# Second layer of all batches but the first with seven quarter products instead of eight, in a fused top-k attention and mixer kernel

## The chip, the cores and the metric

The kernel runs on one core of a Trainium2 chip. The metric is the device time of one execution in microseconds; lower is better. The core's engines work side by side, each through its own list of instructions in order: PE (TensorE) multiplies matrices and writes to PSUM, DVE (VectorE), ACT (ScalarE) and POOL (GpSimd) work on rows of 128 partitions, and SP issues nearly all DMAs of this kernel. [...]

## The reference

Eight batches, eight heads, 576 rows, 64 columns a head. Per head the scores are cut to the 32 largest of each row, then softmax and the product with the values follow; the heads side by side are x, 576 x 512 a batch. Then x is mixed along the rows with a matrix of rank 32, and a two-layer network with ReLU (512 to 2048 to 512) follows, with a residual:

```python
scores = scale * np.matmul(q, k.transpose(0, 1, 3, 2))
kth = np.partition(scores, -top_k, axis=-1)[..., -top_k:-top_k + 1]
scores = np.where(scores >= kth, scores, -1000000000.0)
...
h = x.transpose(0, 2, 1) @ U @ V
u = x + h.transpose(0, 2, 1)
return u + np.maximum(u @ w_ch1, 0.0) @ w_ch2
```

Left out above are the softmax, the product with v and the bridge that puts the heads side by side as x. Everything is fp32.

## The kernel before, in words

**Attention.** It goes by pairs of heads: group g is pair g % 4 of batch g // 4, 32 groups in all. A group has five steps t: four of 128 rows and a last one of 64. The main loop at the end of the file runs over steps n = 5g + t and writes the order of all engines out by hand (a manual schedule: every engine runs its instructions in the order of the program; only the waits are put in automatically, from what reads and writes a tile). In one step stand, from several groups and steps at once: scores of the next step (PE, L323, evicted by ACT, L351), `fold` and `split`, which make a larger half and a smaller half of each row for the search (POOL L390, then DVE L392, then POOL L393), the search for the 32 largest (DVE, `front`: L432 to L463), the marking of what lies below the 32nd (ACT L488, POOL L491), the exponentials (ACT L397), the transposed blocks of the weights (DVE L518, then by SP to DRAM and back: four `away` writes L524 and one `PT` read L528), and the products with the values (PE, L571 to L585, evicted at L594). At t = 0 `load` issues the 21 loads of the next group on SP (L247 to L280). `mixed` (L597) makes the mixer's input u of a pair, transposed: `uT`, 512 x 576 a batch.

**The two layers.** When the last pair of a batch is mixed, `mlp(b)` goes to the list `fillers`. It is a generator that writes one matmul at a time and yields what it costs. `fill`, called eight times in a step, adds a share to `due` and takes matmuls until it is used up; so the layers of one batch are spread between the attention work of the next 20 steps. What is left after the last step runs alone: all of batch 7, and a rest of batch 6.

A batch's 576 columns of uT are cut into two spans of 320 and 256 (`SPAN`). For each span the first layer makes 16 blocks of 128 hidden rows: 4 matmuls (L656) into a PSUM tile `mm`, then ReLU by ACT into SBUF (`hT`, L668). The second layer makes 4 blocks `c` of 128 output rows: 16 matmuls (L675) into an `mm` tile. There are two `mm` tiles, each of 512 fp32 columns, one PSUM bank. The result is copied by ACT and the residual added by POOL (L690, L691); in batch 7 DVE adds from PSUM at once (L688). `turned_back` (L696) transposes a block and stores it: by PE and ACT (L723 to L734), or in batch 7, but for the last block, by DVE and eight or twelve small DMAs (L705 to L717). These jobs wait in the list `late` until the fifth ReLU of the next span or the thirteenth matmul of the next block.

Each fp32 matmul with its weights shows as two matmul records and two weight loads.

**Setting-up.** Weights come as pairs of 32-bit words (`f64_raw`) through three tiles `raw` of 512 KB and are joined on ACT, DVE and POOL in batch 0's attention (L174 to L189).

Of the kernel before, what the change touches and what calls it, by code (L numbers as in the profile page):

```python
# [8 lines left out]
F32 = mybir.dt.float32  # L9
U8 = mybir.dt.uint8  # L10
U32 = mybir.dt.uint32
AF = mybir.ActivationFunctionType
ALU = mybir.AluOpType
# [13 lines left out]
def kernel(  # L27
# [28 lines left out]
    nc = tc.nc  # L56
    B, H, S, D = q.shape
    P = 128
    C = H * D
    R = moe_U.shape[1] // 2  # L60
    F = moe_w_ch1.shape[1] // 2
    NF, NC = F // P, C // P
    NT, TAIL = 4, 64
    MAIN = NT * P
# [9 lines left out]
    NV = 3  # L74

    BLK = 32
    HT = 10
    PE, ACT = mybir.EngineType.PE, mybir.EngineType.Activation
    DVE, POOL, SP = mybir.EngineType.DVE, mybir.EngineType.Pool, mybir.EngineType.SP

# [480 lines left out]
    def values(g, t):  # L561

        PT = PTs.pop((g, t))
        va, vd, vt = (a[g % NV] for a in (vas, vds, vts))
        O = ps_t.tile([P, P], F32, tag="tp", name="O")
        if t == NT:
            den, x = dens[g], xs[g % 2]
            if g not in inverted:
                inverse(g, 2 * NT if g == NPAIR - 1 else 0, 2 * NT + 1)
            for j in range(NT + 1):  # L570
                nc.tensor.matmul(  # L571
                    O,
                    lhsT=PT[:, j],
                    rhs=va[:, :, j, :] if j < NT else vt,
                    start=(j == 0),
                    stop=(j == NT),
                )
            for h in range(2):
                nc.scalar.mul(x[half(h), NT, half(h)], O[half(h), half(h)], den[half(h), 2 * NT :])
            return  # L580
        nc.tensor.matmul(O, lhsT=vd, rhs=PT[:, 2 * NT], start=True, stop=False)  # L581
        PB = PT[:, 0 : 2 * NT].rearrange("p (a h) (c j) -> p h c a j", h=2, c=NT)
        for j in range(NT):
            for h in range(2):
                nc.tensor.matmul(  # L585
                    O[half(h)],
                    lhsT=va[:, h, j, :],
                    rhs=PB[:, h, j] if shared(g, t) else PT[:, NT * h + j],
                    start=False,
                    stop=(j == NT - 1),  # L590
                )
        if t == 0:
            XTs[g] = attn.tile([P, MAIN], F32, tag="XT", name="XT")
        nc.scalar.copy(XTs[g][:, cols(t)], O)  # L594


    def mixed(g, wait, lag=0):  # L597
# [45 lines left out]
        if gi == NPAIR - 1:  # L643
            fillers.append(mlp(b))

    def mlp(b):

        uT = uTs.pop(b)
        late = []
        for chunks, (lo, hi) in zip(PARTS, SPAN):  # L650
            w = hi - lo
            hTs = []
            for f in range(NF):
                ph = ps_m.tile([P, C], F32, tag="mm", name="mm")
                for cc in range(NC):
                    nc.tensor.matmul(  # L656
                        ph[:, 0:w],
                        lhsT=w1[:, cc, f * P : (f + 1) * P],
                        rhs=uT[:, cc, lo:hi],
                        start=(cc == 0),  # L660
                        stop=(cc == NC - 1),
                    )
                    if cc < NC - 1:
                        yield w / C
                if f % 2 == 0:
                    hT = mlpp.tile([P, 2, WIDE], F32, tag="hT", name="hT", bufs=HT)
                    hTs += [hT[:, 0], hT[:, 1]]
                nc.scalar.activation(hTs[f][:, 0:w], ph[:, 0:w], AF.Relu)  # L668
                if f == 4 and late:
                    late.pop()()  # L670
                yield w / C
            for c in range(NC):
                po = ps_m.tile([P, C], F32, tag="mm", name="mm")
                for f in range(NF):
                    nc.tensor.matmul(  # L675
                        po[:, 0:w],
                        lhsT=w2[:, f, c * P : (c + 1) * P],
                        rhs=hTs[f][:, 0:w],
                        start=(f == 0),
                        stop=(f == NF - 1),  # L680
                    )
                    if f == 12 and late:
                        late.pop()()
                    if f < NF - 1:
                        yield w / C
                oT = mlpp.tile([P, WIDE], F32, tag="oT", name="oT")
                if b == B - 1:
                    nc.vector.tensor_tensor(oT[:, 0:w], uT[:, c, lo:hi], po[:, 0:w], ALU.add)  # L688
                else:
                    nc.scalar.copy(oT[:, 0:w], po[:, 0:w])  # L690
                    nc.gpsimd.tensor_tensor(oT[:, 0:w], oT[:, 0:w], uT[:, c, lo:hi], ALU.add)  # L691
                late.append(turned_back(b, chunks, lo, c, oT))
                yield w / C
        late.pop()()

    def turned_back(b, chunks, lo, c, oT):  # L696

# [50 lines left out]
    def fill(k=1):  # L748
# [3 lines left out]
        for _ in range(k):  # L752
            if passes:
                passes.pop(0)()
            if mixing and next(mixing[0], True):
                mixing.pop(0)
            due += share * (SHORT if t == NT else 1) * (EARLY if n <= 2 * ALONE + 2 else 1)
            while due > 0:
                if not fillers:
                    due = 0.0  # L760
# [137 lines left out]
        fill(2)  # L898
    while mixing or fillers:
        fill()  # L900


# [29 lines left out]
```

## Time and profile before

| what | us |
|---|---|
| median of 3 runs (1717.31 to 1718.37) | 1718.03 |
| the profiled execution | 1716.65 |
| its span, first to last instruction | 1714.9 |
| PE busy | 1613.5 |
| DVE busy | 1484.2 |
| ACT busy | 1023.3 |
| POOL busy | 944.9 |
| L656, first layer, 2048 records, busy | 522.8 |
| L675, second layer, 2048 records, busy | 529.5 |
| q1, the queue of nearly all DMAs: share of 16 engines | 37.2% |

A group line in the profile reads: line, engine, operation, tiles written and read, shapes and count; then busy us and mean ns of one; then the idle time of the engine just before, and what ended it. The view of waits gives, for an engine and a line, whose end it waited for: us in total, times, longest. The timeline gives start, length, engine, line, operation and count, with the idle time before in brackets. The view by stretches gives the busy time of PE, PEld (weight loads), DVE, ACT and POOL, then PE's granted clock, the DMA engines' share and GB/s. [...]

### The profile page before, as it was taken

The page shows a single profiled execution, that of the slowest core. Times are in us where ns is not written, and L with a number is a line of the kernel's source. Part 1 is how long each engine was busy: PE and PEld are TensorE (multiplying, and loading weights), DVE is VectorE, ACT ScalarE, POOL GpSimd, SP SyncE. Part 2 cuts the span into 40 slices and gives each one's busy share as a digit, 9 for nine tenths or more (in the row PEclk, how much of TensorE's full clock was granted, in tenths as well). Part 3 has the DMA queues.
Part 4 walks back from the last instruction along what each step waited for, and adds up shares of the span by engine and source line. Part 5 has one row for each costly group of instructions (what it writes and reads, how often), then busy time and mean ns, then how long its engine had stood idle before and what let it go on. Part 6 is the DMA issues. An engine that isn't in the chain of part 4 may idle for free.

```text
span 1714.9 us, 29637 instructions
## 1 busy us (share of the span) xinstructions
PE 1613.5 (94%) x9489; PEld 1219.8 (71%) x9489; DVE 1484.2 (87%) x4317; ACT 1023.3 (60%) x2582; POOL 944.9 (55%) x749
## 2 busy tenths in 40 slices
PE   4666799998999999999999999999999999999999
PEld 2444566787777877788677877788677877788777
DVE  7999989999999999999999999999999999992000
ACT  4888797665656556565656566565655566563100
POOL 4778578666555555565555555565555555552000
PEclk7777899999999999999999999999999999999999
DMA  3322322344444444444444444444444444432010
GB/s 87 95 84 84 84 78 61 77 123 122 108 112 112 117 117 106 112 116 114 115 109 111 119 112 108 114 113 114 111 108 120 118 108 114 106 93 71 3 16 13
DMA packets 275837, 167.37 MB, mean 98 GB/s; under 512 B 173920, under 2 KB 260192, under 8 KB 275680
## 3 DMA queue, kind: packets, MB, share of 16 engines
q1 hardware_dynamic: 274624, 165.20, 37.2%
q8 instruction: 75, 1.23, 0.3%
q14 instruction: 82, 0.67, 0.1%
q10 hardware_dynamic: 1056, 0.26, 0.1%
HBM read 101.42 MB, written 63.96 MB: 96 GB/s over the span
## 4 chain that ended last, share of the span: by engine, by line
PE 71%; DVE 19%; SPq 3%; ACT 2%; issue 2%; DMA 2%; POOL 1%; POOLq 0%; DVEq 0%; ACTq 0%
PE mm L656 27%; PE mm L675 21%; PE sc L323 8%; DVE upper L458 6%; PE O L585 6%; DVE m L463 6%; DVE first L446 2%; SPq L252 2%; PE tp L551 1%; PE O L571 1%; SPq L247 1%; PE up L631 1%; PE O L581 1%; PE tp L546 1%; DVE y L518 1%
## 5 line engine op out<-in xcount | busy, mean ns | idle before, releaser
L675 PE MATMUL mm<-hT,w 128*128 128x256 f32 (+1 forms) x2048 | 529.5, 407 | 0.0
L656 PE MATMUL mm<-uT,w 128*128 128x256 f32 (+1 forms) x2048 | 522.8, 407 | 0.0
L491 POOL TENSOR_TENSOR Ssb<-Ssb,E 128x576 f32<-128x576 f32 x271 | 379.2, 1417 | 246.2 <-ACT E L488 245.8
L656 PEld LDWEIGHTS mm<-uT,w 128*128 128x128 f32 x2048 | 380.0, 191 | 97.6 <-issue 2.6
L675 PEld LDWEIGHTS mm<-hT,w 128*128 128x128 f32 x2048 | 377.9, 191 | 93.0 <-issue 2.9
L463 DVE MAX8 m<-upper 128x8 f32<-128x304 f32 (+1 forms) x864 | 407.7, 508 | 3.6
L458 DVE MATCH_REPLACE8 upper<-m,upper 128x304 f32<-128x304 f32 (+1 forms) x576 | 285.7, 502 | 0.0
L390 POOL TENSOR_TENSOR lower<-Ssb 128x576 uint32<-128x576 uint32 (+1 forms) x135 | 174.3, 1291 | 147.2 <-ACT Ssb L351 51.0
L393 POOL TENSOR_TENSOR lower<-lower,upper 128x576 uint32<-128x576 uint32 (+1 forms) x135 | 174.3, 1291 | 112.2 <-DVE upper L392 104.7
L397 ACT ACTIVATE Ssb<-Ssb,nmax 128x576 f32<-128x576 f32 x286 | 221.5, 777 | 15.3 <-POOL Ssb L468 9.3
L668 ACT ACTIVATE hT<-mm 128x320 f32<-128x320 f32 (+1 forms) x256 | 105.1, 410 | 192.9 <-PE mm L656 191.0
L323 PE MATMUL sc<-qkT 64*128 64x288 f32 x1334 | 211.7, 441 | 8.6 <-ACT Ssb L358 7.8
L488 ACT ACTIVATE E<-Ssb,least 128x576 f32<-128x576 f32 x271 | 198.0, 769 | 5.2
L323 PEld LDWEIGHTS sc<-qkT 64*128 64x128 f32 x1334 | 116.3, 183 | 63.8 <-issue 24.2
L585 PE MATMUL O<-PT,va 128*64 128x128 f32 x2048 | 144.5, 285 | 3.3 <-DMA PT<-away 3.2
L518 DVE STREAM_TRANSPOSE y<-Ssb 128x512 f32<-128x512 f32 x208 | 134.5, 682 | 14.8 <-ACT Ssb L397 14.7
L351 ACT COPY Ssb<-sc 128x576 f32<-128x576 f32 x216 | 127.5, 643 | 32.6 <-PE sc L323 31.0
L688 DVE TENSOR_TENSOR oT<-uT,mm 128x320 f32<-128x320 f32 (+1 forms) x8 | 3.6, 454 | 144.5 <-PE mm L675 144.5
L585 PEld LDWEIGHTS O<-PT,va 128*64 128x64 f32 x2048 | 113.2, 140 | 19.7 <-DMA PT<-away 3.9
L432 DVE MAX8 upper<-lower 128x8 f32<-128x288 f32 x243 | 97.9, 439 | 23.2 <-POOL lower L393 21.2
L392 DVE TENSOR_TENSOR upper<-sc,Ssb 128x576 f32<-128x576 f32 (+1 forms) x135 | 92.0, 682 | 20.7 <-ACT Ssb L351 20.1
L458 DVE MATCH_REPLACE8 upper<-first,upper 128x304 f32<-128x304 f32 x243 | 109.8, 458 | 0.0
(91 smaller groups left out, 1878.7 us busy)
## 6 DMA issues: line engine op xcount, KB each, us to landing
away<-y SPq DMA_DIRECT2D x416, 128.0 KB, 2.4
PT<-away SPq DMA_DIRECT2D x104, 512.0 KB, 3.3
raw<-in_moe_w_ch_dram SPq DMA_DIRECT2D x32, 512.0 KB, 3.9
va<-in_v_dram SPq DMA_DIRECT2D x64, 128.0 KB, 2.2
out_dram<-ob SPq DMA_DIRECT2D x57, 128.0 KB, 2.0
ld<-in_q_dram SPq DMA_DIRECT2D x108, 64.0 KB, 2.6
ld<-in_k_dram SPq DMA_DIRECT2D x108, 64.0 KB, 2.3
ld<-in_q_dram SPq DMA_DIRECT2D x108, 8.0 KB, 2.2
```

Source lines behind the costliest of these rows:

```text
L323: nc.tensor.matmul(out, lhsT=qkT[half(h), 0, cols(t)], rhs=qkT[half(h), 1, lo:hi], start=True, stop=True,)
L390: nc.gpsimd.tensor_tensor(bottom, a.bitcast(U32), b.bitcast(U32), ALU.add)
L393: nc.gpsimd.tensor_tensor(bottom, bottom, top.bitcast(U32), ALU.subtract)
L397: nc.scalar.activation(E, chunk, AF.Exp, bias=nmax, scale=SCALE, accum_out=total)
L458: nc.vector.match_replace(nxt, ms[c], curs[c], NEG)
L463: nc.vector.max(ms[c], curs[c])
L488: nc.scalar.activation(gap, chunks[c], AF.Relu, bias=least[:, c : c + 1], scale=-WIDEN)
L491: nc.gpsimd.tensor_tensor(chunks[c], chunks[c], gap, ALU.subtract)
L518: nc.vector.transpose(y[:, :, h].rearrange("p r c j -> p c r j"), E2[:, a : a + MAIN].rearrange("p (c r j) -> p c r j", c=NT, r=4),)
L585: nc.tensor.matmul(O[half(h)], lhsT=va[:, h, j, :], rhs=PB[:, h, j] if shared(g, t) else PT[:, NT * h + j], start=False, stop=(j == NT - 1),)
L656: nc.tensor.matmul(ph[:, 0:w], lhsT=w1[:, cc, f * P : (f + 1) * P], rhs=uT[:, cc, lo:hi], start=(cc == 0), stop=(cc == NC - 1),)
L675: nc.tensor.matmul(po[:, 0:w], lhsT=w2[:, f, c * P : (c + 1) * P], rhs=hTs[f][:, 0:w], start=(f == 0), stop=(f == NF - 1),)
```

## The change

For batches 1 to 7 the second layer is computed by Winograd's form of Strassen's method. The weights are seen as 2 x 2 quarters (a11, a12, a21, a22; 1024 rows of the inner dimension by 256 output rows), the ReLU output of a span as 2 x 2 quarters (upper and lower 1024 hidden rows, left and right half of the span's columns). Seven products of quarters are made instead of eight. Each has two parts (m = 0, 1), a part has 8 matmuls of half the span's width. Batch 0 keeps its 4 x 16 matmuls (`plain`).

- `sum_weights`, beside batch 1's first layer: POOL makes the sums and differences of the weights' quarters, 16 operations of 512 columns; one, a21 + a22, replaces a21 in SBUF, the other three go to DRAM, six tiles of 512 KB (`sums`). Each operation is a job of `later`, three matmuls after the one before; the DMAs to `sums` and the first three `fetch` jobs follow.
- `fetch`: a ring of three tiles (those of `raw`) brings these six back for each span, by SP; each is asked for two matmuls after the part that used the ring's tile before.
- `halves` and `second`: sums and differences of the quarters of ReLU's output, two operations for each of the 8 pairs of hidden blocks, beside the first layer (whose blocks now come in the order k, k + 8), and two more beside the fourth product; POOL, in batch 7 DVE. A `hT` tile now has five half-width columns: lo_a, lo_b, hi_a, hi_b and T.
- `seven`: the products. All their results lie in the two `mm` tiles, named `left` and `right`: R and one Z in `left`, Q and the other Z in `right`. Q goes on accumulating through four products, and is copied out by ACT after each (the last time, in batch 7, DVE adds from PSUM). R and Z are copied by ACT as well.
- `later` and `tick`: a list of jobs by a count of matmuls. Stores follow twelve matmuls after a block is done; what is left is run at the very end.
- The share of `fill` is 15/16 after step 42. `XT` has one buffer, `oT` four, `hT` eight tiles of 5 x 160 columns (before: ten of 2 x 320).

```diff
-            XTs[g] = attn.tile([P, MAIN], F32, tag="XT", name="XT")
+            XTs[g] = attn.tile([P, MAIN], F32, tag="XT", name="XT", bufs=1)
...
+    def later(wait, job):
+        at = ticks + wait
+        i = sum(p[0] <= at for p in posts)
+        posts.insert(i, (at, job))
+    def tick():
+        nonlocal ticks
+        ticks += 1
+        if posts and posts[0][0] <= ticks:
+            posts.pop(0)[1]()
+    KH, MH = NF // 2, NC // 2
+    def weights(r, c, m):
+        a = (c * MH + m) * P
+        return w2[:, r * KH : (r + 1) * KH, a : a + P]
...
+    def fetch():
+        if coming:
+            tile = ring_tile()
+            nc.sync.dma_start(tile.rearrange("p k c -> p (k c)"), sums[coming.pop(0)])
+            ring.append(tile)
+    def sum_weights():
+        coming.extend(list(range(3 * MH)) * (2 * (B - 1)))
+        wait = 3
+        for m in range(MH):
+            a11, a12, a21, a22 = (weights(r, c, m) for c in range(2) for r in range(2))
+            s4, s2, s3 = tiles = [ring_tile() for _ in range(3)]
+            for k in (slice(0, KH // 2), slice(KH // 2, KH)):
+                for dst, x, y, op in (
+                    (s3, a11, a21, ALU.subtract),
+                    (a21, a21, a22, ALU.add),
+                    (s2, a21, a11, ALU.subtract),
+                    (s4, a12, s2, ALU.subtract),
+                ):
...
...
+    def seven(b, uT, chunks, lo, hi, hTs, first):
+        w = hi - lo
+        h = w // 2
+        adds = nc.vector if b == B - 1 else nc.gpsimd
+        left = ps_m.tile([P, C], F32, tag="mm", name="mm")
+        right = ps_m.tile([P, C], F32, tag="mm", name="mm")
+        R = left[:, 0:h], left[:, h : 2 * h]
+        Q = right[:, 0:h], right[:, h : 2 * h]
+        Z = left[:, 2 * h : 3 * h], right[:, 2 * h : 3 * h]
+        us = [uT[:, c, lo:hi] for c in range(NC)]
+        oTs = []
+        def part(dst, lhs, index, start=False, stop=False, jobs=None):
+            for k in range(KH):
+                nc.tensor.matmul(
+                    dst, lhsT=lhs[:, k], rhs=hTs[k][2][index],
+                    start=(start and k == 0), stop=(stop and k == KH - 1),
+                    skip_group_check=True,
+                )
+                tick()
+                next(jobs, None)
+                if k < KH - 1:
+                    yield h / C
+        def second():
+            for lo_a, lo_b, hi_a, hi_b, T in (hT[2] for hT in hTs):
+                adds.tensor_tensor(lo_a, hi_b, T, ALU.subtract)
+                yield
+                adds.tensor_tensor(hi_a, hi_a, lo_a, ALU.subtract)
+                yield
+        def plus(dst, src):
+            tmp = mlpp.tile([P, WIDE // 2], F32, tag="tmp", name="tmp")
+            nc.scalar.copy(tmp[:, 0:h], src)
+            adds.tensor_tensor(dst, dst, tmp[:, 0:h], ALU.add)
+        for m in range(MH):
+            yield from part(R[m], weights(1, 0, m), 2, start=(m == 0), jobs=first)
...
+        for m in range(MH):
+            yield from part(Q[m], weights(0, 0, m), 0, start=(m == 0), jobs=first)
+            plus(oTs[m][:, 0:h], Q[m])
+            yield h / C
+        for m in range(MH):
+            yield from part(Z[m], weights(0, 1, m), 4, jobs=iter(()))
...
+        jobs = second()
+        for m in range(MH):
+            yield from part(Z[m], ring.pop(0), 3, stop=(m == 0), jobs=jobs)
+            nc.scalar.copy(oTs[m][:, h:w], Z[m])
+            later(2, fetch)
+            yield h / C
+        for m in range(MH):
+            for _ in jobs:
+                pass
+            yield from part(Q[m], ring.pop(0), 0, jobs=jobs)
+            plus(oTs[m][:, h:w], Q[m])
+            adds.tensor_tensor(oTs[m][:, 0:w], oTs[m][:, 0:w], us[m], ALU.add)
+            later(2, fetch)
+            later(12, turned_back(b, chunks, lo, m, oTs[m]))
+            yield h / C
+        for m in range(MH):
+            yield from part(Q[m], ring.pop(0), 1, jobs=jobs)
+            plus(oTs[MH + m][:, h:w], Q[m])
+            later(2, fetch)
+            yield h / C
+        for m in range(MH):
+            c = MH + m
+            yield from part(Q[m], weights(1, 1, m), 2, stop=(m == 1), jobs=jobs)
...
+            later(12, turned_back(b, chunks, lo, c, oTs[c]))
+            yield h / C
+    def halves(adds, lo_a, lo_b, hi_a, hi_b, T):
+        adds.tensor_tensor(T, lo_b, lo_a, ALU.subtract)
+        yield
+        adds.tensor_tensor(lo_b, hi_b, lo_b, ALU.subtract)
+        yield
     def mlp(b):
...
-            due += share * (SHORT if t == NT else 1) * (EARLY if n <= 2 * ALONE + 2 else 1)
+            early = n <= 2 * ALONE + 2
+            due += share * (SHORT if t == NT else 1) * (EARLY if early else 15 / 16)
...
     while mixing or fillers:
         fill()
+    while posts:
+        tick()
```

## The prediction, made before the change was run

> **What bounds the kernel now.** I read the slices of the page first, then one batch's period in stretches of time, its waits, the end of the chain, and last single instructions. (A measurement of this kernel tells about 0.2%, 3.4 us, from no change.)
>
> ```profile
> span 1714.9 us, 29637 instructions
> ...
> PE   4666799998999999999999999999999999999999
> ...
> DVE  7999989999999999999999999999999999992000
> ```
>
> Three stretches: to about 215 us DVE alone is full (batch 0's attention); then PE and DVE both; the last 125 us, batch 7's layers, are PE alone. In the middle one batch takes 193.8 us, and the stretch of just that length shows
>
> ```profile
> 1011.40:1205.20 193.80, 192.49 (x1160) 146.98 (x1160) 184.21 (x565) 118.37 (x305) 111.71 (x89) 1.00 0.43 110
> ```
>
> (busy PE, PEld, DVE, ACT, POOL; granted clock; DMA share; GB/s). PE is idle for 1.3 us of 193.8, DVE for 9.6. PE is the bound; if it gains more than some 9 us, DVE is next. Whatever stops PE inside this stretch lengthens the kernel by as much. The waits of the same stretch (us, times, longest):
>
> ```profile
> POOL Ssb L491 <- ACT E L488: 37.1, 15, 5.5
> ...
> ACT hT L668 <- PE mm L656: 16.6, 23, 1.8
> POOL lower L393 <- DVE upper L392: 15.9, 12, 2.7
> ...
> DVE upper L432 <- POOL lower L393: 1.8, 2, 1.3
> ```
>
> ACT stood waiting for PE at 23 of 32 ReLUs, so a copy from PSUM starts promptly as a rule. POOL's idle 82 us are mostly waits at the head of its queue; L393 stands between two DVE steps.
>
> **The change, part by part.**
>
> *Shorter products, the gain.* The chain ends with pure PE work:
>
> ```profile
> 1620.97 34.45 PE mm L675 x128
> ...
> 1683.05 27.64 PE mm L675 x128
> ```
>
> A matmul is two records here. 320 columns: 34.45/128 = 0.2691 us a record; 256: 0.2159. So 0.00083 us a column and 0.003 fixed; 160 columns cost 0.136, 128 cost 0.1095. That the half width is really to be had, with other weights each time, is seen at 128 columns:
>
> ```profile
> 1569.42 1.05 PE L571 MATMUL O<-va,PT 128*128 128x128 f32 x8
> ...
> 1570.54 0.60 PE L608 MATMUL tp<-ident,XT 128*128 128x128 f32 x4
> ```
>
> One alone takes 0.275 by its row, so (1.05-0.275)/7 = 0.111 and (0.60-0.275)/3 = 0.108 apart. The second layer of a span goes from 64 matmuls to 7 x 16 = 112, 224 records: 30.5 us for 34.45, 24.5 for 27.64. That is -4.0 and -3.1, -7.07 a batch, seven batches: **-49.5**.
>
> *Waits inside the products, the main loss.* Each of the fourteen parts of 8 matmuls ends in a copy (ACT), and all parts write two tiles of one PSUM bank each: R0, R1, Z0 in `left`, Q0, Q1, Z1 in `right`. The order is R0 R1 Q0 Q1 Z0 Z1 Z0 Z1 Q0 Q1 Q0 Q1 Q0 Q1. At eight of the boundaries (R0-R1, Q0-Q1, Z1-Q0, and the five among the last six) the next part writes the bank that the copy of the part before is still reading. Before, every part of a PSUM tile is written and then read, and the two `mm` tiles alternate, so PE never stops there. The trace shows no matmul writing beside a reader in one bank. Bounds: nothing, if both may go on together; else a full turn PE-copy-PE. The nearest row is such a turn at the very end, with DVE as reader:
>
> ```profile
> 1710.72 0.42 DVE L688 TENSOR_TENSOR oT<-uT,mm 128x256 f32<-128x256 f32 x1 [5.71 <-PE mm L675]
> ...
> 1711.19 0.44 PE L723 MATMUL tp<-ident,oT 128*128 128x128 f32 x2 [0.51 <-DVE oT L688]
> ...
> 1712.07 0.39 SPq L729 DMA_DIRECT2D out_dram<-ob  x1
> ```
>
> PE is idle for 0.51: 0.04 to the reader, 0.42, 0.05 back. With a copy of 128 or 160 columns (0.28 to 0.31, below) that is 0.38, and the last record's end lies 0.275-0.1095 = 0.165 behind the place where the next would have started: 0.55 a turn. In the attention stretch ACT is busy in 9 of 32 cases, for some 0.4 us: 0.65. I take the full turn, since wherever the trace of before has a reader and a writer of one tile, one waits for the other. Sixteen turns in batch 7: +8.8. For the other six batches I counted fills: one boundary in sixteen has a step's scores in it, which cover its turn; 6 x 15 x 0.65 = **+58.5**. Ends: 0 and 1.0 a turn (0 and +106).
>
> [...]
>
> *Halves on POOL.*
>
> ```profile
> L552 ACT COPY PT<-tp 128x128 f32<-128x128 f32 x160 | 44.1, 276 | 8.9 <-PE tp L551 8.4
> ...
> L187 POOL TENSOR_TENSOR w<-w,raw 128x512 uint32<-128x512 uint32 x32 | 41.9, 1309 | 36.0 <-DVE w L186 18.4 <-ACT raw L178 8.4 <-ACT least L485 7.5
> ...
> L691 POOL TENSOR_TENSOR oT<-oT,uT 128x320 f32<-128x320 f32 x28 | 24.3, 868 | 29.4 <-ACT oT L690 28.6
> ...
> L691 POOL TENSOR_TENSOR oT<-oT,uT 128x256 f32<-128x256 f32 x28 | 20.5, 731 | 27.0 <-ACT oT L690 26.1 <-DVE upper L458 0.9
> ...
> L187 POOL TENSOR_TENSOR uT<-uT,raw 128x128 uint32<-128x128 uint32 x1 | 0.5, 461 | 18.3 <-ACT least L485 18.3
> ```
>
> 128 columns 0.46, 256 0.73, so 160 about 0.53. A span has 38 more such operations (16 `halves`, 16 `second`, 6 sums): 20.1 + 17.5 us, POOL from 111.7 to 149 a batch. It stays below the period. The first sixteen come two to every eight matmuls of the first layer and fit POOL's idle waits: nothing, and if these are full, 1 us at an L393. The second sixteen come one per matmul while Z is filled the second time: 7.4 to 8.5 us of POOL within two parts, some 6 us of time in which attention wants 3.5. The fifth pair of parts reads what they write (its eighth matmul the fifteenth), so PE is kept some 2 to 3 us in each span, partly beside a turn. A batch, I take 3 (0 if POOL's waits take all; 6 if none of it): **+18** over six batches. Queued behind them are L393 and L491: DVE at L432 and ACT at L397 wait then too; DVE's 9.6 idle us hide it while PE is the later one.
>
> *Ring from DRAM.* Six reads of 512 KB a span; raw weights of that size land in 3.9 us. Three are needed two parts after their issue: 4.4 or 3.5 us of pure PE, 5 to 7 beside attention. They stand in SP's queue:
>
> ```profile
> 1124.70 0.66 SPq L247 DMA_DIRECT2D ld<-in_q_dram  x1
> ...
> 1137.54 0.63 SPq L280 DMA_DIRECT2D vt<-in_v_dram  x1
> ...
> 1140.49 1.89 SPq L524 DMA_DIRECT2D away<-y  x4
> 1144.44 0.34 SPq L528 DMA_DIRECT2D PT<-away  x1
> ```
>
> A read behind the loads of a group (13.5 us, t = 0 and 1) or behind away and PT (4.3 us) comes late. By my count both spans reach the fourth pair, which empties the ring, at t = 1, just behind the loads: 2 to 3 us late, mostly at the place where PE waits for POOL anyway. +1 a batch (0 to 5), +0.5 in batch 7: **+6.5**. The 44 MB more beside 165 MB raise the DMA share by some 0.1; away and PT have 4 us to spare before L581.
>
> *Sums of weights*, once, beside batch 1's first layer: 16 operations of 512 columns, 16 x 1.3 = 21 us on POOL spread over 46 us, with 57% of it taken: **+5** (0 to 12). The second set waits for DMAs of the first out of the ring.
>
> *Tail.* The last posts run after the last add: DVE's transpose of c = 2 and its eight issues (0.46 each, L710) now precede the last DMA, some 4.6 us behind PE's end instead of 1712.07-1710.72 = 1.35, and a little of c = 1: **+4**. Batch 7's sums are DVE's, which is idle: nothing.
>
> *Free otherwise.* hT has the same bytes; XT with one buffer waits for L608, five fills earlier on PE; ACT's 14 short copies for 4 (+2.5 us a span) find 39% idle; the pace 15/16 only keeps a batch's work in 20 steps. If a cover is gone, under 1 us each.
>
> Sum: -49.5+8.8+58.5+18+6.5+5+4 = +51.3 on the profiled execution's 1716.65 (span 1714.9 and 1.75 around it). The median of the runs is 1.4 above that: 1769.3.
>
> **Rivals.**
> A, faster: copies and matmuls share a bank without a turn. Then 1718-49.5+33.5 = 1702, and 1672 if POOL, ring and sums cost nothing. For it: ACT is prompt; against: sixteen boundaries with a reader. It decides where a turn is below 7.07/15 = 0.47 us with the rest free, 0.15 with the rest as priced. 11%, of it 2 near nothing or slower.
> B, POOL becomes the bound: sixteen operations hold L393 back by 3 us, DVE starves, ACT stops at L397 and with it the copies that PE waits for: 6 more a batch, 1805. For it: L393 has 1 to 2 us to spare; against: 23% of POOL idle. 13%.
> C, the ring: reads behind the 13.5 us of loads, 6 more a batch: 1805. 8%.
> D, half-width records wait for their weights (0.19 each by PEld's row): 224 x 0.19 = 43 us a span, +195 in all, over 1900. Against: 0.11 apart above. 2%.
> Forecast 64% (1731 to 1800): its low end has turns of 0.55 and all else free but the tail (+13); the rest, 2%, unthought of.
>
> Range: A is left out but its slow edge, B and C are in; turns of 1.0 with all ends up give 1843, cut to 1830; low 1727. Faster 0.10, within 0.2% 0.02, slower 0.88 (64+13+8+2 and 1).
>
> **What would show it.** After: L675's successor in parts of 16 records, 0.136 and 0.11 apart; at eight of fourteen boundaries PE idle 0.35 to 0.45 for an ACT copy, some 90 us of "PE mm <- ACT" in all; PE's busy time down by some 45; waits of PE for POOL's lo_a and for the ring; POOL near 149 a batch; a batch's period near 201. In the tail a batch 7 of some 127 us. I am wrong if PE shows no wait for those copies (A), if DVE waits for L393 over 10 us a batch (B), or if the DMA of the ring ends PE's long waits (C).

## The result and the profile after

The changed kernel takes 1792.4 us (median of 4 runs, 1792.0 to 1794.7), the kernel before 1718.19 beside it: 1.0436 times as long, interval 1.0418 to 1.0454. That is +74.2 us; the forecast was +51.3, slower. The profiled execution took 1792.0 us (span 1790.2), close to the median. The page of the changed kernel, first its busy times, then the slices of PE and DVE:

```profile
span 1790.2 us, 33269 instructions
...
PE 1619.3 (90%) x10833; PEld 1294.7 (72%) x10833; DVE 1509.0 (84%) x4397; ACT 1049.2 (59%) x2726; POOL 1174.1 (66%) x1221
...
PE   4566899999989999899999999898999989899997
...
DVE  7999988999988989798998979898898979891122
```

One eighth of the second layer's multiplications is gone, yet PE is busy for 1619.3 us, 5.8 more than before, where the prediction had some 45 less. That number misleads in two ways: the records of a dense sequence overlap, so that the last one before a wait counts as busy beyond the place where the next would have started (L755's of 160 columns are 0.30 us long and start 0.136 apart), and a record at half the clock is longer (further down, twelve take 2.99 us for 1.96). PE's row of nines is broken by eights now, and DVE has some eights and sevens where it had nines. No other engine has become full.

The time is lost in every batch. From the first record of one batch's first layer to that of the next (column 7: from batch 7's to the end of the span), in us:

```
batch            0      1      2      3      4      5      6      7
before       221.3  193.8  193.8  193.8  193.8  193.8  186.4  128.5
after        219.3  216.0  204.2  204.3  204.2  203.1  194.0  135.8
difference    -2.0  +22.2  +10.4  +10.5  +10.4   +9.3   +7.6   +7.3
```

One steady batch, batch 3, answers to the 193.8 us shown of before. Its stretch (length; busy PE, PEld, DVE, ACT, POOL; granted clock; DMA share; GB/s):

```profile
848.90:1053.20 204.30, 193.97 (x1355) 158.48 (x1353) 184.73 (x565) 121.67 (x324) 146.69 (x165) 0.98 0.50 138
```

PE's busy time falls short of the stretch by 10.3 us, where it was 1.3. DVE's busy time is the same as before (184.7 against 184.2), so its idle time has gone from 9.6 to 19.6 us. The one wait of PE in the batch shown of before was this (us in total, times, longest):

```profile
PE tp L723 <- POOL oT L691: 1.3, 1, 1.3
```

It is gone. The waits of PE in the stretch after, all of them:

```profile
PE mm L755 <- POOL hT L771: 4.1, 6, 1.9
PE mm L755 <- ACT tmp L779: 3.0, 7, 0.6
PE O L584 <- DMA PT<-away: 0.8, 1, 0.8
PE mm L755 <- ACT oT L785: 0.7, 2, 0.4
PE mm L755 <- ACT oT L825: 0.7, 2, 0.4
PE mm L755 <- ACT least L484: 0.5, 1, 0.5
PE mm L755 <- ACT oT L799: 0.5, 1, 0.5
```

L755 is the matmul of a part, L779, L785, L799 and L825 the copies from its banks, L771 POOL's lo_a of the second sums. ("ACT least" is a copy too; the release is put down to ACT's instruction behind it.) Thirteen waits for ACT, 5.4 us, six for POOL, 4.1, one for a DMA. One turn on the timeline (start, length, engine, line, idle before):

```profile
904.27 0.98 PE L755 MATMUL mm<-hT,w 128*128 128x160 f32 x6
...
905.28 0.29 ACT L785 COPY oT<-mm 128x160 f32<-128x160 f32 x1
...
905.63 1.22 PE L755 MATMUL mm<-hT,w 128*128 128x160 f32 x7 [0.38 <-ACT oT L785]
```

PE ends at 905.25, ACT copies, PE goes on at 905.63: 0.38 idle. The same at batch 7's chain (start, length, what), where nothing lies beside it:

```profile
1711.42 2.46 PE mm L755 x16
1713.90 0.30 ACT tmp L779
1714.20 0.04 issue
1714.25 2.46 PE mm L755 x16
```

And POOL's second sums, with what stands between them in POOL's queue:

```profile
928.99 0.52 POOL L771 TENSOR_TENSOR hT<-hT 128x160 f32<-128x160 f32 x1
929.47 2.77 POOL L490 TENSOR_TENSOR Ssb<-Ssb,E 128x576 f32<-128x576 f32 x2
...
932.68 0.53 POOL L771 TENSOR_TENSOR hT<-hT 128x160 f32<-128x160 f32 x1
...
933.77 1.40 POOL L389 TENSOR_TENSOR lower<-Ssb 128x576 uint32<-128x576 uint32 x1
935.12 0.52 POOL L771 TENSOR_TENSOR hT<-hT 128x160 f32<-128x160 f32 x1
```

The seventh and eighth pair of sums stand behind 2.77 and 1.40 us of attention's work; PE stops for them:

```profile
935.70 0.54 PE L755 MATMUL mm<-hT,raw 128*128 128x160 f32 x2 [1.90 <-POOL hT L771]
936.62 1.73 PE L755 MATMUL mm<-hT,raw 128*128 128x160 f32 x8 [0.38 <-ACT tmp L779]
```

What comes next was in no forecast. L755 by itself in two stretches of 3.4 us, the one that follows this wait and a later one (length; busy PE, PEld; granted clock; DMA share; GB/s):

```profile
937.50:940.90 3.40, 2.99 (x12) 2.59 (x10) 0.50 0.81 247
941.50:944.90 3.40, 1.96 (x12) 1.39 (x10) 1.00 0.45 128
```

The clock granted is half, and twelve records take 2.99 us instead of 1.96 (attention's records stand between them in both stretches). After 400 us such stretches add up to 44.4 us in this execution, and to 6.8 in the one before the change. If a full PE loses half of that time, as the granted 0.50 against 1.00 suggests, that is, by my estimate, up to 18.8 us more than before.

### The profile page after: what moved, and what is told of

It is laid out like the page before. It is cut to its first block, busy times and chain, and to the rows that moved or that the text cites. A ratio compares the mean times of both kernels' runs of the same rounds, so it can differ in the third digit from the quotient of the medians.

```text
span 1790.2 us, 33269 instructions
## 1 busy us (share of the span) xinstructions
PE 1619.3 (90%) x10833; PEld 1294.7 (72%) x10833; DVE 1509.0 (84%) x4397; ACT 1049.2 (59%) x2726; POOL 1174.1 (66%) x1221
## 4 chain that ended last, share of the span: by engine, by line
PE 56%; DVE 19%; POOL 9%; ACT 6%; DMA 4%; SPq 3%; issue 2%; DVEq 0%; POOLq 0%; ACTq 0%
PE mm L852 21%; PE mm L755 16%; DVE upper L457 6%; PE sc L322 6%; DVE m L462 5%; PE O L584 5%; DVE first L445 2%; POOL Ssb L490 2%; POOL lower L389 1%; SPq L246 1%; SPq L251 1%; POOL hT L771 1%; PE up L630 1%; POOL hT L773 1%; DVE y L517 1%
## 5 line engine op out<-in xcount | busy, mean ns | idle before, releaser
L490 POOL TENSOR_TENSOR Ssb<-Ssb,E 128x576 f32<-128x576 f32 x271 | 379.0, 1416 | 128.5 <-ACT E L487 127.0
L755 PE MATMUL mm<-hT,w 128*128 128x160 f32 (+1 forms) x1792 | 248.5, 291 | 22.9 <-ACT tmp L779 12.2
L755 PEld LDWEIGHTS mm<-hT,w 128*128 128x128 f32 x1792 | 231.1, 192 | 36.7 <-ACT tmp L779 18.3
L755 PE MATMUL mm<-hT,raw 128*128 128x160 f32 (+1 forms) x1344 | 215.0, 306 | 42.1 <-POOL hT L771 21.7
L755 PEld LDWEIGHTS mm<-hT,raw 128*128 128x128 f32 x1344 | 188.2, 202 | 59.3 <-POOL hT L771 30.9
L322 PEld LDWEIGHTS sc<-qkT 64*128 64x128 f32 x1334 | 116.4, 184 | 64.6 <-issue 23.9
L431 DVE MAX8 upper<-lower 128x8 f32<-128x288 f32 x243 | 98.5, 442 | 68.2 <-POOL lower L392 68.0
L584 PE MATMUL O<-PT,va 128*64 128x128 f32 x2048 | 144.3, 285 | 10.4 <-DMA PT<-away 10.4
L584 PEld LDWEIGHTS O<-PT,va 128*64 128x64 f32 x2048 | 113.0, 140 | 27.1 <-DMA PT<-away 11.5
```

What stands on the lines that cost most here:

```text
L322: nc.tensor.matmul(out, lhsT=qkT[half(h), 0, cols(t)], rhs=qkT[half(h), 1, lo:hi], start=True, stop=True,)
L490: nc.gpsimd.tensor_tensor(chunks[c], chunks[c], gap, ALU.subtract)
L584: nc.tensor.matmul(O[half(h)], lhsT=va[:, h, j, :], rhs=PB[:, h, j] if shared(g, t) else PT[:, NT * h + j], start=False, stop=(j == NT - 1),)
L755: nc.tensor.matmul(dst, lhsT=lhs[:, k], rhs=hTs[k][2][index], start=(start and k == 0), stop=(stop and k == KH - 1), skip_group_check=True,)
```

## The experiments

All are edits of the changed kernel but the last, which is one of the kernel before. Ratios are against the kernel before on the same chip; where there is none, it is one execution. The executions of one of these kernels lie up to 14 us apart (the changed kernel's 2.7), so small differences are read from the stretches of a batch and not from the times alone.

**Another bank for each m.** R, Q and Z of m = 0 go to `left`, those of m = 1 to `right`, so consecutive parts never write the bank that is being copied. The flags that open and close an accumulation move with them.

```diff
-        R = left[:, 0:h], left[:, h : 2 * h]
-        Q = right[:, 0:h], right[:, h : 2 * h]
-        Z = left[:, 2 * h : 3 * h], right[:, 2 * h : 3 * h]
+        R, Q, Z = ([b[:, i * h : (i + 1) * h] for b in (left, right)] for i in range(3))
...
```

> Edit: all results of m = 0 (R0, Q0, Z0) lie in the tile left, all of m = 1 in right, so that every part writes the other bank than the part before; work, order and waits on data as in the changed kernel. Theory T (the turns PE-copy-PE in one bank are the main loss): the 14 waits of PE for ACT a batch (0.53 each, and 0.10 for the restart) go, 8.4 us a batch in six batches and 9 us in the last, and with them some of the half-clock stretches (up to 3 a batch): 1718 to 1735 us. PE's waits for ACT in the second layer fall below 1 us a batch. Rival P (POOL's sixteen operations before the fifth pair are what sets the pace): PE reaches the fifth pair earlier and waits there for POOL as much longer; 1765 to 1790, with the waits for POOL hT up from 5 to over 10 us a batch.

1756.39 us (1754.3 to 1762.48), ratio 1.0234 [1.0214, 1.0253]: 36 us back, a time between the two ranges that were expected. The waits of PE for ACT in the second layer are gone, but for one, and batch 7 takes 126.7 for 135.8: sixteen turns were 9.1 us, 0.57 each (forecast 0.55), net of one new wait of 0.9 for the ring. In the other batches less came back than the turns had cost. The period fell from 204 to 199 us and not to 195, since other waits grew (waits of PE in batch 4 of this kernel):

```profile
PE mm L753 <- POOL hT L769: 7.0, 8, 1.9
...
```

Without the turns PE reaches the second sums sooner, and POOL makes it wait 7.0 us where it was 4.1. Stretches at half clock added up to 61.4 us, where it was 44.4. So the turns are real and cost what was forecast where they stand alone, but beside attention a part of them lay over POOL's lateness.

**Second sums over two products.** The sums start with Z's first product and come one with every second matmul; the first product of Z doesn't read them.

```diff
...
+        jobs = paced(second())
         for m in range(MH):
-            yield from part(Z[m], weights(0, 1, m), 4, jobs=iter(()))
+            yield from part(Z[m], weights(0, 1, m), 4, jobs=jobs)
...
-        jobs = second()
```

> Edit: the sixteen operations of second are issued one for every second matmul of the third and fourth pair, instead of one for each of the fourth; all else as in the changed kernel. Theory T: POOL's waits of PE (5.1 us and 0.6 for restarts a batch) go or halve, the turns stay; with a half-clock stretch less: 1750 to 1775 us. Rival P: PE and DVE both gain, DVE's wait at lower L392 (9 us a batch) goes too: 1730 to 1750. If POOL's lateness is covered by something else (ring or turns), nothing: 1785 to 1795.

1787.07 us (1780.48 to 1788.51), ratio 1.0399 [1.0374, 1.0424]. Only 5 us, as expected for the case that something else lies over POOL's wait. The waits of batch 3 show why:

```profile
PE mm L755 <- DMA raw<-sum: 4.6, 2, 3.1
PE mm L755 <- ACT tmp L785: 2.6, 6, 0.6
...
PE mm L755 <- POOL hT L771: 0.6, 2, 0.5
```

POOL's wait is nearly gone, and PE waits for the ring's reads instead. They had been as late before: in batch 3 of the changed kernel PE stood waiting for POOL until 935.70, the next read landed at 936.20, and PE came to it at 936.62.

**No reads of the ring,** and **no sums on POOL.** The first kernel leaves the reads out and takes quarters of the weights in SBUF in their place; the second leaves out `halves` and `second`.

```diff
-        if coming:
+        if False:
...
```

> Leaves out the ring: the three products with summed weights read the quarter a12 from SBUF instead; no read of a sum from DRAM, 44 MB less; the sums are still made and written once. Output is not the reference's. If the ring costs what PE's waits for raw show (0 to 1.8 us a batch) and away and PT are late by under 1 us a batch: 1780 to 1790. If its transfers hold up SP or the round trip through DRAM more than that: below 1775.

1786.4 us: -6. The steady period stays at 204, with 4.2 us of POOL's wait; but batch 1 takes 210.2 us for 216.0. So what the reads by themselves cost is the first filling of the ring, in batch 1; the six writes of the sums, which this kernel keeps, are not it. Part of it is the clock: batch 1 stands 17.1 us at half clock in the changed kernel and 6.8 in this one, up to 5 of the 6 us.

```diff
...
-                adds.tensor_tensor(lo_a, hi_b, T, ALU.subtract)
                 yield
-                adds.tensor_tensor(hi_a, hi_a, lo_a, ALU.subtract)
                 yield
...
```

> Leaves out halves and second, all 32 sums and differences of ReLU's quarters a span, on POOL and in batch 7 on DVE; the products read the raw quarters. Output is not the reference's. Theory T: 5.1 us of waits and 0.6 of restarts a batch go, some half clock with them: 1745 to 1765 us, the turns stay. Rival P: 1720 to 1740, as POOL falls back to some 115 us a batch and DVE no longer waits at L431.

1781.1 us: -11, where 27 to 47 were expected. The stretch of batch 4 and its waits:

```profile
1048.50:1250.10 201.60, 190.69 (x1355) 156.53 (x1354) 184.66 (x565) 121.51 (x324) 117.45 (x101) 0.99 0.50 140
```

```profile
PE mm L755 <- DMA raw<-sum: 6.1, 2, 4.2
PE mm L755 <- ACT tmp L777: 2.6, 6, 0.6
...
```

POOL has 29 us less to do, and PE waits for the ring for 6.1 us instead. The two causes lie over each other in time, and taking away either one gives little.

**The products alone.** Banks as above, and neither sums on POOL nor reads of the ring, with `sum_weights` kept.

> Leaves out halves and second and the reads of the sums from DRAM (the products read raw quarters and a12 from SBUF); the bank for each m as in the first experiment. Output is not the reference's. It shows the shorter products with none of the three waits. T2: a batch takes 185 to 188 us, half-clock stretches none or one a batch, 1680 to 1700 us in all. Rival C: still two or more half-clock stretches a batch, over 190 us a batch, 1710 or more.

1678.42 us, 40 us less than the kernel before, in one execution. One batch's stretch:

```profile
993.90:1180.10 186.20, 185.95 (x1355) 154.51 (x1354) 183.71 (x565) 121.48 (x324) 117.57 (x101) 1.00 0.46 118
```

PE is full (185.95 of 186.20) and the period is 7.6 us shorter than before; 1.3 of that is the wait for POOL's oT that the kernel before had. So the products by themselves give 6.3 us a batch where 7.07 were forecast, and PE's busy time is down by 44.7 us over the whole kernel (1568.8 for 1613.5; some 45 forecast). After 400 us only 3.4 us of PE's work stand at half clock, so the shorter records by themselves do not bring it. All that surrounds the products costs 1792.4 - 1678.4 = 114 us. DVE is next to full here, 183.7 of 186.2, so a still shorter PE would gain at most 2.5 us a batch.

**Banks, spread sums, and the reads issued by ACT** instead of SP.

```diff
-            nc.sync.dma_start(tile.rearrange("p k c -> p (k c)"), sums[coming.pop(0)])
+            nc.scalar.dma_start(tile.rearrange("p k c -> p (k c)"), sums[coming.pop(0)])
```

> Edit: the bank for each m of the first experiment, the spread second of the second one, and fetch issued from ACT's queue instead of SP's. Theory T2 (three waits stand one behind the other in the second layer, the turn in the bank, POOL's second, and the ring behind SP's loads; taking one away shows the next): all three go together, PE's waits in the second layer fall below 3 us a batch, no half-clock stretches or one a batch, a batch takes 186 to 190 us: 1685 to 1705 us, faster than both kernels. Rival C (the half clock belongs to the short records themselves, or to DVE as the next bound at 185 us a batch): two or three half-clock stretches a batch stay and a batch takes 191 to 196: 1715 to 1745.

1750.56 us (1742.76 to 1756.44), ratio 1.0187 [1.015, 1.0223]. Above both ranges that were expected, and some 6 us below the banks alone, with times that overlap: a new wait takes the place of the old ones. The longest of batch 4 on the timeline, and SP's own waits in the 39 us around it:

```profile
1232.26 1.98 PE L584 MATMUL O<-PT,va 128*64 128x128 f32 x16 [6.28 <-DMA PT<-away]
```

```profile
SPq L246 <- DMA raw<-sum: 4.3, 1, 4.3
SPq L523 <- DMA raw<-sum: 3.4, 1, 3.4
SPq L278 <- DMA raw<-sum: 3.4, 1, 3.4
...
```

SP's loads and `away` writes now stop until reads that ACT issued have landed; attention's weights come late, and PE waits for them in L584. The load that stood for 4.3 us was issued at 1207.95; it shares no tile with the read that ended its wait, and why it waits for that read no view shows. Here a second issuer moved the wait and didn't remove it.

**Turns alone:** the same without the new banks.

> Edit: the spread second and fetch from ACT's queue, with the banks as in the changed kernel: only the turns are left. T2: 13 to 14 waits for ACT a batch at 0.53 and 0.10 for the restart, a batch takes 195 to 199 us with one or two half-clock stretches: 1740 to 1765 us. If the turns had covered POOL and the ring all along and cost nothing by themselves: below 1725.

1773.31 us, above the 1740 to 1765 expected. In one batch with 14 turns (5.6 us of waits) and 1.4 us of others:

```profile
1045.90:1243.20 197.30, 190.18 (x1355) 155.33 (x1354) 184.72 (x565) 121.95 (x324) 146.50 (x165) 1.00 0.51 141
```

197.3 - 186.2 = 11.1 us is what the turns, with the spread sums and the reads, cost in a batch at full clock; others of this kernel took up to 204.2.

**Another order of the products.** Banks as above; Q, Z, Z, then R of m = 0, Q, R of m = 1, then the rest, so that a product from weights in SBUF stands between those from the ring. The lo_a sums come beside Z's first product, the hi_a sums only beside the last but one Q. SP issues.

```diff
...
+        def lower():
...
         for m in range(MH):
-            yield from part(R[m], weights(1, 0, m), 2, start=(m == 0), jobs=first)
+            yield from part(Q[m], weights(0, 0, m), 0, start=True, jobs=first)
...
+            yield from part(R[m], weights(1, 0, m), 2)
+            plus(oTs[m][:, 0:h], R[m])
...
+            for n in (1, 0):
+                yield from part(Q[n], ring.pop(0), 0)
...
+        jobs = upper()
...
```

> Edit: a bank for each m, and another order of the seven products: Q1 Z1 Z2 R0 Q2 (m = 1, then 0) R1 Q3 Q4, so that parts with weights from SBUF stand between those from the ring and a tile of the ring has three or four parts to come instead of two; lo_a's eight operations on POOL go beside Z1 and hi_a's eight beside Q3, one for every second matmul; fetch on SP as in the changed kernel. Theory T2 (the three waits together are the loss, the products alone gain): PE's waits in the second layer below 3 us a batch, no half clock, a batch 187 to 191 us: 1685 to 1710 us, faster than the kernel before. If the ring's place in SP's queue (blocked by 13.5 us of loads, and blocking them while it waits for PE) is the true limit: a batch 195 to 200, 1735 to 1755.

1758.34 us (1756.83 to 1760.76), ratio 1.0239 [1.0222, 1.0256]: no better than the banks alone, and above both ranges that were expected. POOL's waits are nearly gone, the ring's are not (batch 4):

```profile
PE mm L754 <- DMA raw<-sum: 7.5, 1, 7.5
PE mm L754 <- ACT Ssb L397: 1.4, 1, 1.4
PE mm L754 <- POOL hT L777: 0.9, 2, 0.7
```

One wait of 7.5 us, until 1221.15; the read had landed at 1221.02. SP's timeline shows where it stood, behind all 21 loads of a group, from 1203.19 on:

```profile
1203.19 0.64 SPq L247 DMA_DIRECT2D ld<-in_q_dram  x1
...
1215.90 0.63 SPq L280 DMA_DIRECT2D vt<-in_v_dram  x1
1216.63 1.49 SPq L682 DMA_DIRECT2D raw<-sum  x3
```

**Stores two matmuls behind their block in batch 7,** on top of the order.

```diff
-                later(STORE, turned_back(b, chunks, lo, c, oTs[c]))
+                later(2 if b == B - 1 else 12, turned_back(b, chunks, lo, c, oTs[c]))
...
```

> Edit: as the run with the other order, and in batch 7 the stores follow two matmuls after a block is done instead of twelve, so that they no longer stand together at the end of SP's queue. If the tail's term of the prediction is right (+4 us): 3 to 5 us below the run with the other order. If the stores are hidden: no difference.

1757.77 us (1753.96 to 1761.13), ratio 1.0233 [1.0215, 1.0251]. The stretch from batch 7 is 2.0 us shorter in the profile (124.9 for 126.9); the medians can't tell the two kernels apart.

**The loads two at a time.** On top of the last kernel, `load` becomes a generator; each of the eight `fill` calls of a step issues two of the 21 loads, from batch 2 on, so that a read of the ring can go between.

```diff
...
         for _ in range(k):
+            next(loading, None)
...
-                load(g + 1)
+                loading = load(g + 1)
+                if n < 2 * ALONE:
+                    list(loading)
...
```

> Edit: as the run with the other order and the quicker stores, and from batch 2 on the 21 loads of a group are issued two at a time, one pair for every fill (1.2 us), instead of all at once at t = 0, so that a read of the ring stands behind one pair instead of the rest of 13.5 us. If the ring's place behind the loads makes its late reads (one or two waits, 6 to 8 us a batch, and the half-clock stretches that follow): these waits fall below 2 us a batch, a batch takes 188 to 193 us, 1690 to 1720 us in all. If the reads are late for another reason (the away and PT round trip, or the release of the ring's tile by PE): 1745 to 1760 as before.

1728.93 us (1726.7 to 1733.13), ratio 1.0065 [1.0043, 1.0087]: 29 us from the issue of the loads alone, though less than expected. The longest wait of batch 4 is 3.1 for 7.5:

```profile
PE mm L755 <- DMA raw<-sum: 3.8, 2, 3.1
PE mm L755 <- POOL hT L778: 1.1, 2, 0.7
...
```

**A pair at every second fill,** and q and k transposed a step later, at t = 2.

```diff
...
-            if t == 1 and g + 1 < NP:
+            if t == (1 if n < 2 * ALONE else 2) and g + 1 < NP:
                 ready = prep(g + 1)
...
-        if t == 1:
+        if t == 2:
             list(loading)
```

> Edit: as the run with the loads in pairs, but a pair for every second fill, and the transposition of the loaded q and k one step later (t = 2), so that SP has room between the loads. If SP's work at t = 0 and 1 (16 of 21 loads at its full rate) is what still makes the ring late: PE's waits for raw fall from 4 us a batch to under 1.5, a batch takes 189 to 192 us, 1700 to 1716 us, as fast as the kernel before or a little faster. If DVE, at 184 us of work a batch and with its own waits at lower L393, is the next bound: a batch stays at 193 to 195 and the time at 1722 to 1732.

1704.99 us (1702.89 to 1705.69; five rounds), ratio 0.9921 [0.9908, 0.9935]: 0.8% below the kernel before; the interval ends short of 1. A batch's stretch and all its waits of PE above 0.5 us:

```profile
1014.50:1203.90 189.40, 187.02 (x1355) 154.82 (x1354) 183.74 (x565) 120.92 (x324) 145.95 (x165) 1.00 0.53 149
```

```profile
PE mm L757 <- POOL hT L780: 1.6, 3, 0.7
PE O L588 <- DMA PT<-away: 0.8, 2, 0.6
```

No wait for the ring is left, and no half clock in this batch. The period of batches 2 to 5, 189.4 to 191.2, is 2.6 to 4.4 below that of before. Batch 1, beside which the weights' sums are made and the ring is first filled, takes 202.3 us, 8.5 more than before.

**The kernel before with its loads paced in the same way.**

> Edit: the kernel before, with nothing of the change, but its loads paced as in the last run (a pair for every second fill from batch 2 on, q and k transposed at t = 2). If pacing only makes room for the ring: no difference to the kernel before, 1714 to 1722 us. If the gain of the last run over the kernel before belongs to the pacing itself: 1700 to 1710.

1717.63 us (1716.78 to 1718.51), ratio 1.0001 [0.9991, 1.001]. Without the ring nothing waits behind the loads, and pacing them gives nothing. So the gain of the kernel above is that of the seven products, once most of what they brought with them is out of the way; 27 us are still lost against the products alone (1705.0 for 1678.4).

## Why the prediction was right, and where it fell short

The side and the range were right (1727 to 1830), and the main loss is the one that it named; the sum was 23 us too low. That it came so near is in part luck, because its terms do not add. Without turns its own sum is 1702 (rival A), and the kernel with other banks, which has none, took 1756: POOL's sums and the ring's reads, priced at 24.5 together, are worth 78 us there against the products alone, up to 29 of them through the half clock (half of 61.4 less 3.4, an estimate as above). In the changed kernel the turns lay over much of that. Its terms, as the prediction put them:

*Shorter products, -49.5.* Somewhat too high: 6.3 us a batch for 7.07. The sum for the kernel with the products alone would be -49.5 + 4 for the tail + 5.5 for the weights' sums (below) = -40.0; it measured -39.9, but with 9.8 us of the old wait for oT gone, which the prediction left out.

*Turns, 58.5 + 8.8.* Right in size and kind. Over the six batches beside attention L755 stood waiting for ACT 79 times; against a dense sequence (0.136 and 0.110 a record) it started 45.9 us late for them, 0.58 each, and the second record behind each wait another 0.10 late, which the prediction did not have: 54 in all. Thirteen turns a batch were not covered where fifteen were counted. In batch 7 the same count gives 8.7 and 1.7 for the second records; the bank experiment gave 9.1, net of its new wait for the ring. The "some 90 us" of such waits that were to show it was a slip: PE's idle time for these copies is 38 us in all, as 106 turns of 0.38 would have told.

*Halves on POOL, 18.* Too low. By the same count the lateness is 26.7 us in 30 waits, and 3 for the restarts. The step "7.4 to 8.5 us of POOL within two parts, some 6 us of time in which attention wants 3.5" was the right one; 3 of its 0 to 6 a batch should have been 5. DVE's L431, which the prediction let POOL hold up, did wait in the steady batch, just short of the 10 us that were to show rival B (us, times, longest):

```profile
DVE upper L431 <- POOL lower L392: 9.0, 7, 2.9
```

It was 1.8. These waits did not set the pace: the kernel with paced loads keeps all of POOL's sums and runs a batch in 189 to 191 us. POOL's busy time was right: 146.7 a batch for 149.

*Ring, 6.5.* The sum is about right, 4.6 us in four waits and 6 without the reads, but not the reason it was so small. The reads do stand behind the loads as rival C had it, up to 7.5 us in the kernel with another order; in the changed kernel PE is then waiting for POOL anyway. When POOL's wait is taken away, 4.6 to 6.1 us a batch come out.

*Sums of weights, 5.* Too low by half: batch 1 takes 216.0 us, 11.8 above the steady 204.2. The kernel with the products alone, which keeps these sums, has 191.7 against 186.2: 5.5, as forecast. The kernel without the reads has 210.2 against 204 in batch 1. The other 6 us are the ring's first reads, for which this step had no price, with the half clock that comes with them. The prediction gave attention's own `away` and `PT` 4 us to spare beside the ring's transfers; here they stand behind the reads in SP's queue, and that was not enough. SP's timeline of batch 1 in the changed kernel:

```profile
494.84 2.82 SPq L681 DMA_DIRECT2D raw<-sum  x3
497.71 2.43 SPq L523 DMA_DIRECT2D away<-y  x4
504.56 0.34 SPq L527 DMA_DIRECT2D PT<-away  x1
```

In batch 1 the reads wait at the queue's head for the writes of the sums (4.5 us in three waits); the `away` writes are issued 0.05 us behind the last of them, `PT` follows, and PE stops:

```profile
508.18 1.97 PE L584 MATMUL O<-PT,va 128*64 128x128 f32 x16 [4.32 <-DMA PT<-away]
```

*Tail, 4.* Right: the last DMA was issued at 1787.51, 4.6 us behind the end of PE's last product at 1782.88, for the 4.6 forecast and the 1.35 of before. Batch 7 in all is +7.3 for +6.2. The "some 127 us" named for it was a slip: 128.5 and +6.2 give 134.7, and 135.8 came.

*What was missing: the half clock.* No term held it. With 37.6 us more of it than before it explains up to 18.8 of the 23 us; in batches 2 to 5 it is 23.9 us, so up to 3.0 a batch of the 10.4 that were measured for 6.7 forecast. The rest is POOL (+12) and the first reads (+6), against turns that came out 4 lower and the 1.3 us a batch of the old oT wait, which is gone. These shares overlap and don't add up to 23: the clock's part holds up to 5 of the first reads' 6. The range's upper end has a slip too: the ends of the terms as stated add up to 1857, not 1843; it was cut to 1830 either way.

*Rivals.* A fell: PE waits at every uncovered turn. D fell: the records stand 0.136 apart, and the weight loads, 0.19 each, do not hold them back. B and C did not decide in the changed kernel, but both mechanisms are there, one behind the other, and with the turns gone they are what is left of the loss.

## What to carry to other kernels

Count the turns first: where a product accumulates into parts of one bank and each part is copied out, PE lost about 0.6 us a copy here, and giving consecutive parts different banks is a small edit that was worth 36 us. Where two waits end near each other, taking one away shows the other: taking away POOL's wait, the ring's reads or POOL's sums alone gave 5, 6 and 11 us, and only the kernel with neither these nor the turns showed that the products were worth 40, and so that it was worthwhile to go on. When a transfer is added to a queue that issues bursts (21 loads in 13.5 us), pace the burst: that turned +2.4% into -0.8%, on top of an order of products that keeps two reads from being needed at once and that had given nothing by itself. No run paces the loads without that order.

## What was not expected of the hardware

**Half clock after small waits.** After 400 us, the fourteen executions profiled (both kernels and the twelve) have 98 stretches with a granted clock of 0.5. In each execution they begin on one fixed grid of 3.413 us and last one, two or three of its steps. I put PE's idle time in each step at full clock beside the clock of the next:

```
PE idle in a step of 3.413 us    next step at half    next step at full
below 1.3 us                             1             over 5100
1.3 to 1.6                               7                    32
1.6 to 1.9                               5                    24
1.9 to 2.2                              23                     2
above 2.2                               62                     0
```

So it is the idle time within a step that goes with it, with a border somewhere near 1.9 us, and not one long wait: in five of the ten stretches of the changed kernel no single wait before it was above 0.8. One step with four waits of 0.46 for POOL (1231.0 to 1234.4, 1.6 us by this count) was followed by half clock, while the 14 turns of 0.38 in the batch shown of the kernel with turns alone, farther apart, were followed by none. That the idle time is the cause, and not something that goes with it, is argued from this table; no experiment set the idle time by itself. Against a rival, that the short records themselves bring it, stands the kernel with the products alone, which has the same records and one such step.

The longest wait that stood ahead of the stretch at 937.5 was 1.90 us. By the table, steps with 1.9 us or more of idle time in all were followed by half clock 85 times in 87; ahead of four of the changed kernel's ten stretches it was 1.4 to 1.6 us.

**The price of a turn.** With a copy of 0.29 to 0.30 us PE stood idle for 0.38, as built from the turn at the very end of the kernel before. Added to it are the 0.16 us by which a record's end lies behind the place of the next start (0.30 less 0.136) and 0.10 us before the second record; no row of before had shown that last one. The wait itself is one that the program puts in, from what reads and writes a tile. The parts share a tile and a bank, and no run separates the two, or shows what a bank shared without a wait would do.
